# Four first loads on the ScalarE queue behind one memset, and another tile for the gate ahead of W_in

## The chip, the core and the metric

The kernel runs on one core of a Trainium2 chip. A core has TensorE (matrix products), VectorE, ScalarE, GpSimd and SyncE, which work side by side, each through its own instructions in order, and which wait for one another through semaphores. Sixteen DMA engines move data between the chip's memory (HBM) and the on-chip SBUF. SyncE and ScalarE issue DMAs through a hardware queue each, GpSimd through a software queue; all three run on the same sixteen DMA engines. The metric is the time of one execution on the device in microseconds (us), given as the median of several runs.

## The reference

A gated linear recurrence gives the input of a feed-forward layer. All inputs are float32: q, k, v and alpha are 4 x 8 x 768 x 48 (batch, heads, sequence, width of a head), W_in is 384 x 2048, W_out is 2048 x 384.

```python
for t in range(S):
    state = alpha[:, :, t, :, None] * state + np.einsum('bhd,bhe->bhde', k[:, :, t], v[:, :, t])
    y[:, :, t] = np.einsum('bhd,bhde->bhe', q[:, :, t], state)
...
x = y.transpose(0, 2, 1, 3).reshape(B * S, H * D)
h = x @ w_in
g = 0.5 * h * (1.0 + np.tanh(c * (h + 0.044715 * h * h * h)))
out = g @ w_out
```

## The kernel before

**Tiling.** The sequence is cut into 6 chunks of 128 tokens. A chunk of one batch entry is a unit; two units make a pair, and there are 12 pairs, two for each chunk. In a chunk the recurrence is written as an attention with a running product of alpha: ScalarE takes the logarithm of alpha (`ln`, L359), TensorE sums it over the tokens by a product with a triangular matrix (`cum`, L346 to L380), ScalarE makes the exponentials `b` and `binv` and the decay at the chunk's end `bend`, VectorE multiplies q by b and k by binv (`qp` and `kp`, L418). TensorE transposes both (`t`, L428), ScalarE or VectorE copies the result to SBUF (`ev`, L446), TensorE forms the products of q and k (`attn`, L489), VectorE masks them (`mask`, L496), TensorE multiplies by v (`y`, L543 and L546), and the state is carried on (`kv`, `st`). The output of a unit is transposed (`tx`, `xe`) and goes into layer 1 (`l1`, L572, product with W_in), GELU on ScalarE (L578) and layer 2 (`l2`, L591, product with W_out).

**Names.** `qp0.1` is the second `qp` of pair 0, and so on; `l10.3` is step 3 of layer 1 of block 0. A step of layer 1 covers two of the 16 column tiles of W_in, so steps 0 and 1 read part 0 of W_in, 2 and 3 part 1, 4 and 5 part 2, 6 and 7 part 3.

**Order.** A planner puts the tasks of each engine in order with costs and due times, but up to about the middle of pair 3 the order is written out by hand in the string `FIRST`: `A:ln0.0` means "ScalarE, next, ln0.0", with P, V, G and S for TensorE, VectorE, GpSimd and SyncE. Layer 1 of block 0 stands there in the order l10.0, l10.1, l10.3, l10.2, l10.5, l10.4, l10.6, l10.7, between the steps of pair 1. The planner's table of landing times (`LANDED`) is written out too. Each engine runs its instructions in that order.

**Loads.** The alpha, q and k of pairs 0 and 1 are loaded unit by unit through the hardware queues, 192 KB each: the table `RINGS` numbers them load.0 to load.11 (0 and 1 are alpha of pair 0, unit 0 and 1; 2 and 3 are q and k of unit 0; 4 and 5 are q and k of unit 1; 6 and 7 alpha of pair 1; 8 and 9 q and k of its unit 0; 10 and 11 those of its unit 1). Those in `BY_ACT` are issued by ScalarE, the others by SyncE. Everything else (v, W_in in 4 parts, W_out in 4 parts, and all loads from pair 2 on) goes through GpSimd's queue in the order of `LOADS`. A "gate" in that list is a copy of one element of a loaded tile by GpSimd (L314): GpSimd's queue stands until that tile has landed. `gatea 0 1` stands ahead of v of pair 0 and reads alpha of pair 0, unit 1; `gatek 0 1` stands ahead of W_in part 0 and reads k of pair 0, unit 1. Behind it in GpSimd's queue are W_in part 0, v of pair 1, W_in parts 1 to 3, W_out parts 0 and 1, and the loads of pair 2.

SyncE's last four loads of pair 1 each also wait until an earlier hardware load has landed, since they use its semaphore again: load.8 waits for load.0, load.9 for load.1, load.10 and load.11 for the third and the fourth hardware load of the program's order.

`run` (L865) first fills constants on VectorE and GpSimd and then emits the tasks in the order.

Of the kernel before, what the change touches and what calls it, by code (L numbers as in the profile page):

```python
# [7 lines left out]
F32 = mybir.dt.float32  # L8
# [163 lines left out]
class _Kernel:  # L172
# [3 lines left out]

    SPLIT = (2,)
    EARLY = (0, 1)
    LOADS = ('gatea 0 1', 'v0', 'gatek 0 1', 'in 0', 'v1', 'in 1', 'in 2', 'in 3', 'out 0', 'out 1', '2a', 'out 2', '2b', 'out 3', '3', '4', '5', '6', '7', '8', '9', '10', '11')

    PACKED, CUM_FF, R = (0, 1), (0, 1), 4
    RINGS = (('a', 0, 0, 1), ('a', 0, 1, 2), ('q', 0, 0, 1), ('k', 0, 0, 1), ('q', 0, 1, 2), ('k', 0, 1, 2),
             ('a', 1, 0, 1), ('a', 1, 1, 2), ('q', 1, 0, 1), ('k', 1, 0, 1), ('q', 1, 1, 2), ('k', 1, 1, 2))
    BY_ACT = (2, 3,)

    FIRST = """
        A:table.0 A:load.2 A:load.3 S:load.0 S:load.1 S:load.4 A:ln0.0 S:load.5 P:fill.7 P:cum0.0 A:ln0.1 G:gate.0 G:load.12 S:load.6 P:cum0.1 A:b0.0 S:load.7
        A:bend0.0 V:qp0.0 A:binv0.0 A:binv0.1 S:load.8 V:kp0.0 P:fill.2 P:t0.0 A:b0.1 V:ev0.0 P:fill.1 P:t0.1 S:load.9 A:ev0.1 V:qp0.1 S:load.10 A:bend0.1
        P:fill.3 P:attn0.0 V:kp0.1 G:gate.1 S:load.11 P:t0.2 G:load.13 V:mask0.0 A:ev0.2 P:t0.3 G:load.14 V:mask0.1 A:ev0.3 P:fill.1 P:t0.4 V:ev0.4 P:fill.1
        P:attn0.1 A:ln1.0 G:load.15 P:t0.5 V:mask0.3 P:cum1.0 A:ev0.5 G:load.16 V:vb0.0 A:ln1.1 V:end0.0 P:y0.0 V:mask0.2 G:load.17 P:kv0.0 A:binv1.0 P:cum1.1  # L190
# [428 lines left out]
    def tasks(self):  # L619
# [30 lines left out]
        for r, m, lo, hi in self.RINGS:  # L650
            loads[r, m, lo] = loads[r, m, hi - 1] = s.add(
                "load", {"ACT" if n in self.BY_ACT else "SP": W["ring_issue"]}, n, self.load(r, *pairs[m], lo, hi), land=(W["ring_v" if r == "v" else "ring"] * (hi - lo) // 2 if n else W["begin"]))
            n += 1
        for step in self.LOADS:
            if step[0] == "v":
# [209 lines left out]
    def run(self):  # L865
        nc, C = self.nc, self.C
        self.tasks()
        nc.vector.memset(self.zero, 0.0)
        nc.vector.memset(self.ones, 1.0)
        make_upper_triangular(nc, self.ut_h, val=1.0, diag=True)  # L870
        make_identity(nc, self.ident)
        nc.vector.memset(self.half, 0.0)
        for o in range(2):
            nc.vector.memset(self.half[64 * o:64 * o + 64, o:o + 1], 1.0)
        nc.vector.tensor_reduce(self.blk, self.ident.rearrange("p (g j) -> p j g", j=4), axis=mybir.AxisListType.X, op=ALU.max)
        same = self.blk[:, None, :].to_broadcast([C, C // 4, 4])
        nc.vector.tensor_tensor(self.ut_blk[1].rearrange("p (g j) -> p g j", j=4), self.ut_h.rearrange("p (g j) -> p g j", j=4), same, op=ALU.mult)
        nc.vector.tensor_tensor(self.ut_blk[0], self.ut_blk[1], self.ident, op=ALU.subtract)
        for i in range(max(self.BUFS[n] for n in self.ring)):
            for n in self.ring:  # L880
                if i < self.BUFS[n]:
                    nc.vector.memset(self.ring[n][i][:, :, :, self.D:64], 0.0)
        nc.vector.tensor_copy(self.ut, self.ut_h)
        order = self.s.order()
        for t in order:
            if t.load == LN_EXP:
                self.act_set(LN_EXP)
            t.emit(t.engine)
# [30 lines left out]
```

## Time and profile before

| | us |
|---|---|
| median of 9 runs | 177.43 |
| lowest and highest run | 176.85, 178.6 |
| the profiled execution | 176.79 |
| its span, first to last instruction | 175.0 |

TensorE's clock was granted in full (mean 1.000). The page lists each engine's busy time in the span, the chain of work that ended last, and the groups of instructions. An engine's busy share is an average over the whole span; for a change at the start the timeline of the start has to be read. In it, the landings of the first loads, as issue plus time to landing:

| load | issued by | issue, us | to landing, us | landed |
|---|---|---|---|---|
| alpha, pair 0, unit 0 | SyncE | 0.74 | 3.1 | 3.8 |
| q, pair 0, unit 0 | ScalarE | 0.77 | 3.5 | 4.3 |
| k, pair 0, unit 0 | ScalarE | 1.52 | 5.4 | 6.9 |
| q, pair 0, unit 1 | SyncE | 2.20 | 5.2 | 7.4 |
| k, pair 0, unit 1 | SyncE | 2.85 | 5.1 | 7.95 |
| v, pair 0 | GpSimd | 5.14 | 6.5 | 11.6 |
| k, pair 1, unit 0 | SyncE | 5.48 | 6.0 | 11.5 |
| W_in, part 0 | GpSimd | 8.53 | 6.0 | 14.5 |

From about 3 us on the DMA engines are busy nearly all the time (the share of them that is busy is 0.88 to 1.26 in every microsecond from 3 to 14; it can pass 1 because packets overlap).

### The profile page before, as it was taken

To read this page: it belongs to the slowest core of one execution; us is meant where nothing else is said; L and a number is where in the kernel's file an instruction comes from. 1 tells how busy PE (TensorE), PEld (TensorE's weight loads), DVE (VectorE), ACT (ScalarE), POOL (GpSimd) and SP (SyncE) were. 2 spreads that over 40 slices of the span, in tenths; PEclk is the share of its full clock that TensorE was granted. 3 is DMA by queue.
4 is the path that set the end of the run, shared out by engine and by line. 5 is a ranking of instruction groups with operands and counts; after the bars stand their busy time and mean duration, and the time that the engine had idled before them with its cause. 6 is when DMAs were issued, how large, how long until landed. Compare 5 with 4: busy or idle time off the path is not lost.

```text
span 175.0 us, 4439 instructions
## 1 busy us (share of the span) xinstructions
PE 169.9 (97%) x1845; PEld 134.9 (77%) x1845; DVE 96.5 (55%) x191; ACT 128.7 (74%) x213; POOL 57.6 (33%) x64
## 2 busy tenths in 40 slices
PE   7899999999999999999999999999999999999993
PEld 2567998667987896897798698698697697796973
DVE  6599820357888993895697997485426405000000
ACT  4677999666978668669788967977988984481941
POOL 2497348986645766566720000000000000000000
PEclk9999999999999999999999999999999999999999
DMA  4999999999999999999999993261270360401102
GB/s 140 294 269 227 209 244 234 242 208 208 250 263 194 248 251 218 226 226 198 193 275 218 194 153 102 59 171 43 47 187 28 90 165 4 119 16 49 45 0 90
DMA packets 49620, 28.86 MB, mean 165 GB/s; under 512 B 37696, under 2 KB 46016, under 8 KB 49600
## 3 DMA queue, kind: packets, MB, share of 16 engines
q0 software_dynamic: 26464, 17.70, 61.2%
q1 hardware_dynamic: 22592, 10.49, 24.8%
q10 hardware_dynamic: 544, 0.39, 0.8%
q8 instruction: 14, 0.23, 0.6%
q14 instruction: 6, 0.05, 0.1%
HBM read 25.17 MB, written 4.72 MB: 171 GB/s over the span
## 4 chain that ended last, share of the span: by engine, by line
PE 92%; DMA 3%; DVE 1%; ACT 1%; issue 1%; DVEq 0%
PE hT L572 36%; PE acc L591 36%; PE at L489 4%; PE qkT_ps L428 4%; DMA k<-in_k_dram 3%; PE yps L546 3%; PE kv L506 2%; PE yps L543 2%; PE cum L378 2%; PE xT_ps L560 1%; PE cum L380 1%; ACT qkT L446 1%; PE idle L289 1%; DVE kp L418 1%; PE k_ps L454 0%
## 5 line engine op out<-in xcount | busy, mean ns | idle before, releaser
L572 PE MATMUL hT<-xT,w_in 128*128 128x256 bf16 x576 | 69.4, 273 | 0.0
L578 ACT ACTIVATE gT<-hT 128x512 bf16<-128x512 f32 x96 | 56.3, 600 | 17.7 <-PE hT L572 14.3
L591 PE MATMUL acc<-w_out,gT 128*128 128x384 bf16 (+3 forms) x416 | 69.0, 313 | 0.0
L572 PEld LDWEIGHTS <-w_in 128*128 128x128 bf16 x576 | 61.1, 113 | 1.6
L591 PEld LDWEIGHTS <-gT 128*128 128x128 bf16 x416 | 36.9, 97 | 19.2
L496 DVE TENSOR_TENSOR atm<-at,ut 128x512 bf16<-128x512 f32 x48 | 30.1, 683 | 12.7 <-PE at L489 12.6
L418 DVE TENSOR_TENSOR qp<-q,b 128x768 bf16<-128x768 f32 (+1 forms) x15 | 11.9, 796 | 13.4 <-ACT b L407 13.4
L418 DVE TENSOR_TENSOR kp<-k,binv 128x768 bf16<-128x768 f32 (+1 forms) x15 | 11.9, 792 | 11.1 <-ACT binv L407 10.6
L603 ACT COPY ot<-acc 128x384 f32<-128x384 f32 (+3 forms) x17 | 7.4, 439 | 13.0 <-PE acc L591 12.9
L308 POOL DMA_DIRECT2D k<-in_k_dram x11 | 12.2, 1107 | 8.2 <-DMA vb<-in_v_dram 2.5
L308 POOL DMA_DIRECT2D a<-in_alpha_dram x11 | 12.2, 1114 | 5.7 <-DMA w_in<-in_moe_w_in_dram 1.4
L308 POOL DMA_DIRECT2D vb<-in_v_dram x11 | 12.1, 1104 | 5.6 <-PE qkT_ps L428 1.4
L308 POOL DMA_DIRECT2D q<-in_q_dram x11 | 12.2, 1108 | 5.4 <-DMA w_out<-in_moe_w_out_dram 1.0
L407 ACT ACTIVATE b<-cum 128x768 bf16<-128x768 f32 (+1 forms) x15 | 10.3, 684 | 3.2 <-PE cum L380 2.3
L280 ACT ACT_TABLE_LOAD x9 | 11.5, 1283 | 0.9 <-PEq L903 0.7
L578 ACT ACT_TABLE_LOAD x9 | 11.5, 1283 | 0.2
L407 ACT ACTIVATE binv<-cum 128x768 bf16<-128x768 f32 (+1 forms) x15 | 10.2, 681 | 0.2 <-PE cum L350 0.2
L528 DVE TENSOR_TENSOR stmp<-kv,st 128x384 f32<-128x384 f32 x16 | 8.9, 553 | 2.1 <-PE kv L506 2.0
L446 ACT COPY qkT<-qkT_ps 128x512 bf16<-128x512 bf16 (+1 forms) x9 | 6.5, 728 | 4.0 <-PE qkT_ps L428 4.0
L553 DVE CAST x<-yps 128x384 bf16<-128x384 f32 x12 | 6.7, 557 | 4.9 <-PE yps L546 4.9
L531 DVE TENSOR_TENSOR st<-stmp,ends 128x384 bf16<-128x384 f32 x16 | 8.9, 558 | 0.6
L546 PE MATMUL yps<-vb,atm 128*128 128x48 bf16 x192 | 8.7, 183 | 0.1
(64 smaller groups left out, 155.1 us busy)
## 6 DMA issues: line engine op xcount, KB each, us to landing
out_dram<-ot SPq DMA_DIRECT2D x19, 192.0 KB, 5.4
a<-in_alpha_dram POOLq DMA_DIRECT2D x9, 384.0 KB, 12.2
q<-in_q_dram POOLq DMA_DIRECT2D x9, 384.0 KB, 11.6
k<-in_k_dram POOLq DMA_DIRECT2D x9, 384.0 KB, 11.8
vb<-in_v_dram POOLq DMA_DIRECT2D x9, 192.0 KB, 11.7
w_in<-in_moe_w_in_dram POOLq DMA_DIRECT2D x4, 384.0 KB, 8.3
w_out<-in_moe_w_out_dram POOLq DMA_DIRECT2D x4, 384.0 KB, 11.0
out_dram<-ot SPq DMA_DIRECT2D x9, 96.0 KB, 1.8
```

The source lines that it names most:

```text
L280: nc.scalar.add_instruction(mybir.InstLoadActFuncSet(name=nc.get_next_instruction_name(), act_func_set_id=i, engine=mybir.EngineType.Activ ...
L308: dma(u[t][:, lo:hi].rearrange("t b h d -> t (b h) d"), src.rearrange("b h s d -> s (b h) d")[c * C:(c + 1) * C])
L407: self.nc.scalar.activation(u[n].rearrange("t i h d -> t i (h d)")[:, lo:hi], cum, AF.Exp, scale=1.0 if n == "b" else -1.0)
L418: self.nc.vector.tensor_tensor(out, rows, b, op=ALU.mult)
L446: self.copy(e)(t, ps)
L496: self.nc.vector.tensor_tensor(u["atm", i][:, o], u["at", i][o], self.ut[:, None, :].to_broadcast([self.C, self.H // 2, self.C]), op=ALU.mult)
L528: nc.vector.tensor_tensor(s, acc, old, op=ALU.add)
L531: nc.vector.tensor_tensor(new.rearrange("f p (o d) -> f (p o) d", o=2), acc.rearrange("f p (o d) -> f (p o) d", o=2), ends, op=ALU.mult)
L546: nc.tensor.matmul(y[:, h, :], u["atm", i][:, h % 2, h // 2, :], u["vb"][:, i, h, :], start=c == 0, stop=True, skip_group_check=True)
L572: self.nc.tensor.matmul(h[:, s], w_in[:, j, nt % 4 + s], self.xT[c % self.NX][:, j, lo:hi].rearrange("p g t -> p (g t)"), start=j == 0, st ...
L578: return lambda e: self.nc.scalar.activation(self.gT[c % self.NG][:, nt:nt + 2, lo * self.C:hi * self.C], f.pop(("h", c, lo, nt)), AF.Gelu ...
L591: self.nc.tensor.matmul(f["acc", c, b][:, lo:hi], self.gT[c % self.NG][:, nt, b * self.C:(b + 1) * self.C], self.w_out[:, nt, lo:hi], star ...
```

## The change

Four things are edited.

- `BY_ACT` is (2, 3, 4, 5) instead of (2, 3), and `FIRST` begins with load.4 and load.5 on ScalarE: q and k of both units of pair 0 are now issued by ScalarE, right after its table load and ahead of ln0.0. SyncE issues the four alphas of pairs 0 and 1 one after another, and then q and k of pair 1.
- In `run` the tile of q of pair 0 is made before the planner's tasks, and VectorE writes a zero to one element of each partition of it, after the constants zero and ones. The first load into that tile therefore waits for this memset, and with it the three that stand behind it on ScalarE's queue.
- The gate ahead of W_in reads k of pair 1, unit 0 (`gatek 1 0`) instead of k of pair 0, unit 1.
- The semaphores used again follow the new order: load.10 now waits for q of pair 0, unit 0, and load.11 for k of pair 0, unit 0.

The order of instructions on TensorE, and the order of the rest on the other engines, is the same. (The lines behind the new ones count two further.)

```diff
-    LOADS = ('gatea 0 1', 'v0', 'gatek 0 1', 'in 0', 'v1', 'in 1', ...
+    LOADS = ('gatea 0 1', 'v0', 'gatek 1 0', 'in 0', 'v1', 'in 1', ...
...
-    BY_ACT = (2, 3,)
+    BY_ACT = (2, 3, 4, 5)
...
     FIRST = """
-        A:table.0 A:load.2 A:load.3 S:load.0 S:load.1 S:load.4 A:ln0.0 S:load.5 P:fill.7 P:cum0.0 A:ln0.1 G:gate.0 ...
+        A:table.0 A:load.2 A:load.3 A:load.4 A:load.5 S:load.0 S:load.1 A:ln0.0 P:fill.7 P:cum0.0 A:ln0.1 G:gate.0 ...
...
         make_upper_triangular(nc, self.ut_h, val=1.0, diag=True)
+        first = self.p[0, 0]["q"] = self.tile("q", [C, 2, self.H, self.D], F32)
+        nc.vector.memset(first[:, 0, 0, 0:1], 0.0)
         make_identity(nc, self.ident)
```

More of the change, by code (lines that the diff above doesn't have):

```diff
@@ L178 @@
     EARLY = (0, 1)
-    LOADS = ('gatea 0 1', 'v0', 'gatek 0 1', 'in 0', 'v1', 'in 1', 'in 2', 'in 3', 'out 0', 'out 1', '2a', 'out 2', '2b', 'out 3', '3', '4', '5', '6', '7', '8', '9', '10', '11')
+    LOADS = ('gatea 0 1', 'v0', 'gatek 1 0', 'in 0', 'v1', 'in 1', 'in 2', 'in 3', 'out 0', 'out 1', '2a', 'out 2', '2b', 'out 3', '3', '4', '5', '6', '7', '8', '9', '10', '11')
     PACKED, CUM_FF, R = (0, 1), (0, 1), 4
@@ L183 @@
              ('a', 1, 0, 1), ('a', 1, 1, 2), ('q', 1, 0, 1), ('k', 1, 0, 1), ('q', 1, 1, 2), ('k', 1, 1, 2))
-    BY_ACT = (2, 3,)
+    BY_ACT = (2, 3, 4, 5)
     FIRST = """
-        A:table.0 A:load.2 A:load.3 S:load.0 S:load.1 S:load.4 A:ln0.0 S:load.5 P:fill.7 P:cum0.0 A:ln0.1 G:gate.0 G:load.12 S:load.6 P:cum0.1 A:b0.0 S:load.7
+        A:table.0 A:load.2 A:load.3 A:load.4 A:load.5 S:load.0 S:load.1 A:ln0.0 P:fill.7 P:cum0.0 A:ln0.1 G:gate.0 G:load.12 S:load.6 P:cum0.1 A:b0.0 S:load.7
         A:bend0.0 V:qp0.0 A:binv0.0 A:binv0.1 S:load.8 V:kp0.0 P:fill.2 P:t0.0 A:b0.1 V:ev0.0 P:fill.1 P:t0.1 S:load.9 A:ev0.1 V:qp0.1 S:load.10 A:bend0.1
```

## The prediction

> **What bounds the kernel now.** I read the page's busy shares first, then the chain of waits (whole, and for the first 13.5 us), then timelines by engine up to 36 us, then the DMA view cut to short stretches.
>
> ```profile
> PE 169.9 (97%) x1845; PEld 134.9 (77%) x1845; DVE 96.5 (55%) x191; ACT 128.7 (74%) x213; POOL 57.6 (33%) x64
> PE 92%; DMA 3%; DVE 1%; ACT 1%; issue 1%; DVEq 0%
> ```
>
> TensorE is busy 97% of the 175.0 us span and is 92% of the chain that ended last; in the list of waits TensorE has one of 1.2 us at the very start, three of 0.2 to 0.3 up to 10 us, and none in the dense part. So whatever delays TensorE once its dense stretch has begun (about 16.5 us) comes out at the end undiminished, and only the first 23 us, where it still depends on loads, can change the time. The chain there:
>
> ```profile
> 0.74 0.75 ACT L280
> ...
> 1.52 5.39 DMA k<-in_k_dram
> ...
> 7.00 0.57 DVE kp L418
> 7.62 0.40 PE qkT_ps L428 x4
> ```
>
> Columns are start, length, piece. The one long load on the chain is k of unit 0 (ScalarE issues it at 1.52, it lands at 6.91). VectorE's kp stood ready 0.52 us for it. Then the gate and W_in on GpSimd, and the products that read W_in (start, length, engine, line; the bracket is idle time):
>
> ```profile
> 8.06 0.18 POOL L314 COPY gate<-k 128x1 f32<-128x1 f32 x1 [1.64 <-DMA k<-in_k_dram]
> 8.53 0.74 POOL L321 DMA_DIRECT2D w_in<-in_moe_w_in_dram  x1 [0.29 <-issue]
> 9.26 1.18 POOL L308 DMA_DIRECT2D v<-in_v_dram  x1
> 10.43 2.25 POOL L321 DMA_DIRECT2D w_in<-in_moe_w_in_dram  x3
> ```
>
> ```profile
> 16.52 0.82 PE L572 MATMUL hT<-xT,w_in 128*128 128x256 bf16 x6
> ...
> 19.14 0.83 PE L572 MATMUL hT<-xT,w_in 128*128 128x256 bf16 x6
> ...
> 19.97 1.47 PE L572 MATMUL hT<-xT,w_in 128*128 128x256 bf16 x12
> ...
> 22.48 6.71 PE L572 MATMUL hT<-xT,w_in 128*128 128x256 bf16 x60
> ```
>
> The DMA view by issue gives the landings: parts 0 to 3 of W_in take 6.0, 7.8, 8.9 and 10.0 us from issues at 8.53, 10.43, 11.18 and 11.93, so they land at 14.5, 18.2, 20.1 and 21.9. By the hand order l10.0 (16.52) is first to need part 0, l10.3 (19.14) part 1, l10.5 (the second six of the twelve at 19.97, so about 20.6) part 2, l10.6 (22.48) part 3. **The slack is 2.0, 0.9, 0.5 and 0.5 us.** That is the number this case turns on.
>
> **The change, part by part.**
>
> *The order of instructions.* TensorE's order is unchanged. VectorE gains one tiny memset near 1.15 us (the 128x1 memset of the ones took 0.06 us): it lies under the wait for alpha and costs nothing.
>
> *The hold.* Load q of unit 0 now waits for that memset, so ScalarE issues from about 1.2 us instead of 0.77. Alpha 0 loses its competitor for 0.4 us; alpha 1 no longer shares with q. I expect alpha 0 at about 3.5 (was 3.84) and alpha 1 at 4.4 to 4.9 (was 4.95).
>
> *Four issues on ScalarE instead of two.* Its two took 0.72 and 0.88 us; SyncE's take 0.61 to 0.74. Four from 1.2 us end between 3.6 (4 x 0.61) and 4.6 (0.72 + 3 x 0.88); I take 4.1, the middle, because each of its two rows overlapped one of SyncE's and the new ones overlap too. Queued behind them is ln of unit 0 (3.83 before): so about +0.3, between 0 and +0.75, and the earlier alpha is not used. Cover: binv of unit 0 ends at 6.33 and kp waits for k until 6.91, so 0.6 us of such a delay is hidden if k lands as before. If k came sooner, this would be late next.
>
> *Where q and k travel.* k of unit 0 stays the fourth load in order of issue; q and k of unit 1 fall from fifth and sixth to sixth and eighth, since SyncE now issues both alphas of pair 1 right after those of pair 0. The next rows are the two hardware queues in the stretch from 5 to 7 us, SyncE's q1 and ScalarE's q10:
>
> ```profile
> q1 hardware_dynamic: 715, 0.52, 86.0%
> q10 hardware_dynamic: 88, 0.06, 11.5%
> ```
>
> While k of unit 0 was still under way on ScalarE's queue, that queue moved 88 packets beside SyncE's 715. The Trainium skill (DMA: Bandwidth & Descriptors, "Issuing engines are not separate DMA queues") says that DMAs of several engines interleave on the same 16 engines, so spreading them saves only sequencer time. By that rule landing follows total bytes: the sixth and eighth landings of before, 7.95 and 9.07. By the row, ScalarE's queue may get less than its turn. Unit 1's q is used at 8.08 and k at 8.57. By the rule kp of unit 1 is 0.5 late; of that 0.4 hides where k's transposed copy on ScalarE (10.0) waits behind q's, leaving +0.1 to +0.2. By the row it may be 1 to 2 us late. Against that, k of unit 0 may come 0.2 to 0.6 earlier on its own queue. I take the head at +0.2, with ends of -0.4 and +2.0.
>
> *The new release of W_in.* The text in the code is "gatek 1 0": the tile read is k of pair 1, unit 0, on SyncE's queue. Before it landed at 11.5 (issue 5.48, 6.0 us) and the gate stood on k of unit 1 of pair 0, 7.95. In the new order ten loads of 0.197 MB and v of pair 0 (0.393 MB) stand up to it: 2.36 MB. Summing the GB/s of before by microsecond (123 from 2 us, then 356, 289, 261, 322, 321, 330, 301) that much is through at 10.2; landing lags the packets by 0.5 to 1.2. I take 10.9, ends 10.2 and 11.6. From landing to the issue of W_in took 0.58 (7.95 to 8.53), so part 0 is issued at 11.5 instead of 8.53: +3.0. Behind the gate in GpSimd's queue stand v of pair 1, W_in 1 to 3, W_out 0 and 1, and the loads of pair 2; all move with it.
>
> *How much of those 3.0 us comes back.* Part 0 took 6.0 us before, sharing with SyncE's queue until about 12.2. The Trainium skill (same page, "Anatomy of one DMA — SWDGE (gpsimd) path") gives about 2.0 us plus bytes over 436 GB/s; with the 0.786 MB read that is an estimate of 3.8 us. The rows say more: v of pair 0, issued at 5.14, showed its first packet at 8.25, and the landings of W_in parts are 1.85 us apart when nothing else runs. First packet 2.1 to 3.1 after the issue, 1.85 of packets, 0.5 of lag: 4.5 to 5.5. I take 4.7, nearer the short end because the queue is empty by then. Part 0 lands at 11.5 + 4.7 = 16.2, **1.7 later**; by the page it would be 15.3 and 0.8 later. The parts behind come back to back at the pace of before, so all are 1.7 late. The same seen from the engines: SyncE's loads end near 11.5 to 12 and W_in's first packet comes near 13.6, a hole of about 1.7 where before there was none.
>
> *The sum.* Part 1 stalls TensorE by 1.7 - 0.9 = 0.8, part 2 and part 3 raise this to 1.7 - 0.5 = 1.2. A late head moves the need for W_in by as much, so the two don't add: the larger counts, 1.2 against 0.2. By the page's figure it would be 0.8 - 0.5 = 0.3. v of pair 1 (16.7, first used at 18.07, slack 1.4) adds 0.3 at most, inside the same 1.2. W_out parts 0 and 1 have slack of 5.3 and about 3.3 and stay covered.
>
> The profiled execution took 176.79 us (175.0 of span and 1.8 around it): 176.79 + 1.2 = 178.0. The median of the nine runs, 177.43, is 0.64 above it, so the median to expect is 177.43 + 1.2 = **178.6 us**.
>
> **The rivals.**
>
> *Hidden.* k of pair 1 lands at 10.2 and a lone W_in load takes 3.8 to 4.3: part 0 is 0.1 to 0.6 late, within the slack of 0.5, and the head stays. 177.4. For it: the page's figure, and that alphas and rows reach SyncE's queue earlier. Against: v of pair 0 still shares the stretch before, and no load on GpSimd's queue in this trace landed in under 6.0 us.
>
> *ScalarE's queue is starved.* With up to eight loads on SyncE's queue, q and k of unit 1 come at the share shown above and land 2 us later (k at 10 or after). kp of unit 1, the second attention product, its mask, and v's cast behind it on VectorE move, and TensorE's dense part starts 1.5 to 2.0 later: 179.2. For it: 88 against 715. Against: by 7 us that was only the tail of one load.
>
> *Faster.* Place: kp of unit 0. With the alphas alone on the wire and k on a queue of its own, k lands by 6.3; ScalarE's four issues end by 3.7; kp starts 0.5 earlier and everything behind follows. Price: -0.5, 176.9; more isn't to be had, because binv ends at 6.33. It decides only if W_in is at most 0.0 us late, since an earlier head eats the slack of 0.5. For it: the 0.52 us wait at kp is real. Against: three conditions at once, one of them against the 3.0 us later issue.
>
> **How the numbers follow.** 0.3% is 0.53 us, about what a measurement of this kernel can tell from no change: 176.9 to 177.96. Forecast (W_in late, +0.6 to +2.5): 0.60. Hidden: 0.20, nearly all within 0.3%. Starved: 0.12. Faster: 0.08. Slower 0.71, same 0.21, faster 0.08. The range of 177.1 to 180.0 leaves out the faster case and a W_in more than 3 us late.
>
> **What would show it.** Right: the gate's copy starts near 11, W_in's first issue near 11.5, a dent in DMA share between 12 and 13.5, and TensorE waiting at hT for W_in at about 19 to 23 us, in sum near 1 us, with the rest unchanged and shifted. ln of unit 0 starts at 4.0 or later. Wrong: no wait on W_in; or kp of unit 1 well after 9.1, which is the starved case; or the gate before 10. If the gate's copy is near 11 and W_in still lands by 15, the term of 4.7 us was too large.

## The result, and the profile after

The changed kernel takes **179.02 us** (median of 18 runs, 178.42 to 179.94). The kernel before, run beside it and since, has a median of 177.23 us in 54 runs. The ratio is **1.0101, 95% interval 1.0081 to 1.0121**: 1.8 us slower. The forecast was 178.6 us, in a range of 177.1 to 180.0. The ratios below leave out two slow runs, 180.75 us in experiment 2 and 179.78 in experiment 6, each over 1.5% above the fastest of its kernel.

The page of the changed kernel, on an execution of 178.94 us: the span, TensorE's busy time, the hardware queues' packets, and the chain of waits by engine and line.

```profile
span 177.2 us, 4440 instructions
...
PE 170.1 (96%) x1845; PEld 135.0 (76%) x1845; DVE 96.5 (54%) x192; ACT 128.7 (73%) x213; POOL 58.0 (33%) x64
...
q1 hardware_dynamic: 22048, 10.10, 23.5%
q10 hardware_dynamic: 1088, 0.79, 1.4%
...
PE 90%; DMA 5%; DVE 1%; ACT 1%; issue 1%; SPq 0%
PE hT L572 36%; PE acc L591 34%; PE at L489 4%; PE qkT_ps L428 4%; DMA a<-in_alpha_dram 3%; PE yps L546 3%; DMA xT<-x 2%; PE kv L506 2%; PE yps L543 2%; PE cum L378 2%; PE xT_ps L560 1%; PE idle L289 1%; ACT qkT L446 1%; PE cum L380 1%; PE k_ps L454 0%
```

TensorE does the same work (170.1 us against 169.9), so the 2.2 us of longer span are waits. Two loads went over to ScalarE's queue (q10 has 1088 packets, and had 544). The long load on the chain is no longer k of unit 0 but an alpha. The next lines are GpSimd's timeline of the changed kernel (start, length, engine, line):

```profile
6.50 0.19 POOL L314 COPY gate<-a 128x1 f32<-128x1 f32 x1 [4.68 <-DMA a<-in_alpha_dram]
...
9.95 0.38 POOL L314 COPY gate<-k 128x1 f32<-128x1 f32 x1 [2.04 <-DMA k<-in_k_dram]
10.41 0.75 POOL L321 DMA_DIRECT2D w_in<-in_moe_w_in_dram  x1
11.15 1.18 POOL L308 DMA_DIRECT2D v<-in_v_dram  x1
12.33 2.26 POOL L321 DMA_DIRECT2D w_in<-in_moe_w_in_dram  x3
```

W_in part 0 is issued at 10.41 instead of 8.53. Parts 1 to 3, with 7.7, 8.8 and 10.0 us to landing from 12.33, 13.08 and 13.84, land at 20.0, 21.9 and 23.8: 1.8 to 1.9 later than before. TensorE's timeline of the changed kernel shows what that does, and one wait far behind:

```profile
17.66 0.81 PE L572 MATMUL hT<-xT,w_in 128*128 128x256 bf16 x6
...
20.28 0.83 PE L572 MATMUL hT<-xT,w_in 128*128 128x256 bf16 x6
...
21.11 1.66 PE L572 MATMUL hT<-xT,w_in 128*128 128x256 bf16 x12
...
23.83 6.74 PE L572 MATMUL hT<-xT,w_in 128*128 128x256 bf16 x60
...
102.65 0.82 PE L572 MATMUL hT<-xT,w_in 128*128 128x256 bf16 x6 [0.70 <-DMA xT<-x]
```

Layer 1 begins 1.14 late (17.66 against 16.52), and l10.6, the first to need part 3, 1.35 late (23.83 against 22.48). The 0.21 added on the way are W_in: the twelve products at 21.11 take 1.66 instead of 1.47, and l10.6 begins at the landing of part 3 (23.8), though no bracket shows a wait. Read by itself, this page seems to say that the late second alpha made most of the loss and W_in little. The alpha (ScalarE's `ln`, the idle time in the bracket):

```profile
6.47 0.52 ACT L359 ACTIVATE la<-a 128x384 f16<-128x384 f32 x1 [2.02 <-DMA a<-in_alpha_dram]
```

It had started at 4.99. So two theories stood after this page. **Two-limits theory:** the gate costs the time, as forecast; in this execution a late head (the work ahead of layer 1) merely lay beside it, since a late head moves the need for W_in too and only the larger of the two counts. **Head theory:** the moved issues delay the second alpha, and that is the cost. Beside them, the forecast's rule (lateness of part 3 less its slack of 0.5) could be tested by doses.

### The profile page after: what moved, and what is told of

Read it like the earlier page. It is cut to its first block, busy times and chain, and to the rows that moved or that the text cites. A ratio compares the mean times of both kernels' runs of the same rounds, so it can differ in the third digit from the quotient of the medians.

```text
span 177.2 us, 4440 instructions
## 1 busy us (share of the span) xinstructions
PE 170.1 (96%) x1845; PEld 135.0 (76%) x1845; DVE 96.5 (54%) x192; ACT 128.7 (73%) x213; POOL 58.0 (33%) x64
## 3 DMA queue, kind: packets, MB, share of 16 engines
q10 hardware_dynamic: 1088, 0.79, 1.4%
## 4 chain that ended last, share of the span: by engine, by line
PE 90%; DMA 5%; DVE 1%; ACT 1%; issue 1%; SPq 0%
PE hT L572 36%; PE acc L591 34%; PE at L489 4%; PE qkT_ps L428 4%; DMA a<-in_alpha_dram 3%; PE yps L546 3%; DMA xT<-x 2%; PE kv L506 2%; PE yps L543 2%; PE cum L378 2%; PE xT_ps L560 1%; PE idle L289 1%; ACT qkT L446 1%; PE cum L380 1%; PE k_ps L454 0%
## 5 line engine op out<-in xcount | busy, mean ns | idle before, releaser
L578 ACT ACTIVATE gT<-hT 128x512 bf16<-128x512 f32 x96 | 56.4, 599 | 18.8 <-PE hT L572 15.3
L280 ACT ACT_TABLE_LOAD x9 | 11.5, 1283 | 0.9 <-PEq L905 0.7
L578 ACT ACT_TABLE_LOAD x9 | 11.5, 1283 | 0.2
## 6 DMA issues: line engine op xcount, KB each, us to landing
w_out<-in_moe_w_out_dram POOLq DMA_DIRECT2D x4, 384.0 KB, 10.9
```

Of the source, the lines that this page charges most:

```text
L280: nc.scalar.add_instruction(mybir.InstLoadActFuncSet(name=nc.get_next_instruction_name(), act_func_set_id=i, engine=mybir.EngineType.Activ ...
L578: return lambda e: self.nc.scalar.activation(self.gT[c % self.NG][:, nt:nt + 2, lo * self.C:hi * self.C], f.pop(("h", c, lo, nt)), AF.Gelu ...
```

## The experiments

All ratios are to the kernel before on the same chip, with 95% intervals.

**1. The gate alone.** The kernel before, no issue moved, nothing held:

```diff
-    LOADS = (... 'gatek 0 1', 'in 0', ...
+    LOADS = (... 'gatek 1 0', 'in 0', ...
```

> The kernel before with the one edit at the gate: W_in waits for k of pair 1, unit 0. Two-limits theory (the later of the head and of W_in sets the time): the head is as before (second ln at about 5.0, kp at 7.0), the gate opens near 11.3, W_in is issued near 11.8 and each part lands 2.3 to 3 later, so TensorE waits for W_in by 1.8 to 2.5 in sum: 179.0 to 179.7, as slow as the changed kernel or slower. Head theory (the late second alpha alone costs the time, W_in is covered): no change from before.

Measured: 179.98 us, ratio 1.0171 (1.0132 to 1.0209), the slowest of all. GpSimd's and TensorE's timelines of this kernel:

```profile
10.82 0.18 POOL L314 COPY gate<-k 128x1 f32<-128x1 f32 x1 [4.43 <-DMA k<-in_k_dram]
11.28 0.74 POOL L321 DMA_DIRECT2D w_in<-in_moe_w_in_dram  x1 [0.29 <-issue]
```

```profile
17.62 0.85 PE L572 MATMUL hT<-xT,w_in 128*128 128x256 bf16 x6 [0.93 <-DMA w_in<-in_moe_w_in_dram]
...
21.60 0.85 PE L572 MATMUL hT<-xT,w_in 128*128 128x256 bf16 x6 [1.17 <-DMA w_in<-in_moe_w_in_dram]
...
23.48 0.84 PE L572 MATMUL hT<-xT,w_in 128*128 128x256 bf16 x6 [0.21 <-DMA w_in<-in_moe_w_in_dram]
...
26.03 6.20 PE L572 MATMUL hT<-xT,w_in 128*128 128x256 bf16 x55 [0.50 <-DMA w_in<-in_moe_w_in_dram]
```

Here the alphas and k of pair 0 are about as early as before, or earlier, and TensorE waits 2.8 us for W_in in four places; its list of waits names no other load. The span is 178.5: 3.5 longer, and l10.6 is 3.55 late. The head theory, which had expected no change, falls as the only cause. The time even lies above the range expected.

**2. The changed kernel with the old gate.** The same line the other way round.

> The changed kernel with the old gate: W_in waits for k of pair 0, unit 1, which landed at 8.85. Two-limits theory: the second alpha still lands at 6.4, so the head is 1.1 late, W_in is issued near 9.5 and is about 0.9 late, covered: TensorE starts layer 1 near 17.65 and the sum is +1.1 over before (178.3), only 0.2 to 0.3 under the changed kernel. W_in theory (the gate alone costs the time): back within 0.3 of before.

Measured: 178.02 us, ratio 1.0065 (1.0039 to 1.0090). By its size (+1.1) this is the number of the two-limits theory, but not by its reason: in the profiled execution, at 177.1 the lowest of the 14, the second alpha landed at 4.9 and layer 1 began at 16.45, no later than before. The stricter theory, that the old gate brings the time back within 0.3, is refuted. A second execution of each of the two kernels was profiled.

> The changed kernel with the old gate once more, one look, because the first look's time (177.1) was the lowest of 14. At the usual 178.0 the trace should show what the first one did not: the second alpha at 6 or later or k of unit 1 after 9 (head theory), or W_in parts 2 and 3 about 1 late and TensorE waiting for them (W_in theory), or a wait for a transposed x near 100.

This execution took 178.42. ScalarE's and GpSimd's timelines of it:

```profile
5.64 0.52 ACT L359 ACTIVATE la<-a 128x384 f16<-128x384 f32 x1 [1.19 <-DMA a<-in_alpha_dram]
```

```profile
9.30 0.18 POOL L314 COPY gate<-k 128x1 f32<-128x1 f32 x1 [2.22 <-DMA k<-in_k_dram]
9.76 0.74 POOL L321 DMA_DIRECT2D w_in<-in_moe_w_in_dram  x1 [0.28 <-issue]
```

k of unit 1, now last in ScalarE's queue, lands 1.2 later than before (9.2 against 7.95). The old gate stands on that very tile, so W_in is late here too (9.76 against 8.53) and TensorE waits 0.7 us for it at l10.3 and l10.5. Layer 1 itself begins at 17.16, 0.64 late. Head and W_in are both late in this execution; W_in is the later one, since l10.6 begins (24.18) when part 3 lands (24.1).

> The changed kernel once more, one look. If the late second alpha (6.4) belongs to the change: it lands at 6.0 to 6.5 again. If it is a matter of one execution: at 4.9 to 5.1, with W_in's parts still 1.5 to 2 late and the time 178.4 to 179.4 all the same.

Measured 179.6 us. TensorE's timeline of this second execution of the changed kernel:

```profile
17.40 0.81 PE L572 MATMUL hT<-xT,w_in 128*128 128x256 bf16 x6
18.50 0.82 PE L572 MATMUL hT<-xT,w_in 128*128 128x256 bf16 x6
20.92 0.84 PE L572 MATMUL hT<-xT,w_in 128*128 128x256 bf16 x6 [0.74 <-DMA w_in<-in_moe_w_in_dram]
21.77 0.82 PE L572 MATMUL hT<-xT,w_in 128*128 128x256 bf16 x6
22.87 0.84 PE L572 MATMUL hT<-xT,w_in 128*128 128x256 bf16 x6 [0.28 <-DMA w_in<-in_moe_w_in_dram]
23.76 0.83 PE L572 MATMUL hT<-xT,w_in 128*128 128x256 bf16 x6
25.30 6.74 PE L572 MATMUL hT<-xT,w_in 128*128 128x256 bf16 x60 [0.38 <-DMA w_in<-in_moe_w_in_dram]
```

Same instructions, another picture: the second alpha was there at 5.25 instead of 6.4, W_in was issued at 10.92, and TensorE waited 1.4 us for W_in. The alpha at 6.4 was a matter of one execution; the late W_in was there in both. The two are coupled: k of pair 1, on which the gate stands, uses the semaphore of the second alpha again, and it was issued right behind that alpha's landing, at 6.47 in the first execution and at 5.27 in the second.

**3. W_in released early in the changed kernel.** If the moved issues cost anything by themselves, it must be left when W_in is early.

```diff
-    LOADS = (... 'gatek 1 0', 'in 0', ...
+    LOADS = (... 'gatek 0 0', 'in 0', ...
```

> The changed kernel with W_in released by k of pair 0, unit 0 (lands near 6.5 to 6.9), so that W_in is early and only the head is left. Two-limits theory: layer 1 starts 0 to 1.1 late as the second alpha lands early or late in that execution, TensorE never waits for W_in, sum +0.6 to +1.1 over before (177.5 to 178.1). If W_in is all of it: equal to before within 0.3. A new competitor (W_in's packets beside q and k of unit 1) could add: then kp of unit 1 after 9.5 and +1.5.

Measured: **177.29 us, ratio 1.0009 (0.9985 to 1.0033)**: nothing measurable is left of the loss. TensorE's list of waits (us in total, times, longest) and GpSimd's issue in this kernel:

```profile
PE idle L289 <- DVE half L874: 1.2, 1, 1.2
PE k_ps L454 <- ACT qkT L446: 0.5, 1, 0.5
PE cum L346 <- ACT la L359: 0.4, 1, 0.4
PE yps L546 <- DVE vb L389: 0.2, 1, 0.2
PE qkT_ps L428 <- DVE xT L564: 0.2, 1, 0.2
```

```profile
7.92 0.74 POOL L321 DMA_DIRECT2D w_in<-in_moe_w_in_dram  x1
```

No wait for W_in. The execution profiled was the slowest of 13, though (178.9 us, with layer 1 beginning at 18.7), and so late a head needs W_in later: the parts landed at 15.5 to 23.1, each 1.0 to 1.2 later than in the kernel before. So the trace doesn't show an early W_in, and the verdict rests on the median: one edit at the gate, with all moved issues and the hold in place, takes the loss away.

**4. The same early release in the kernel before.**

> The kernel before with the same earlier release of W_in. W_in is covered before already (slack 0.5), so an earlier W_in gains nothing: 0 to +0.3 over before by more sharing for q and k of pair 1. If W_in's slack is often used up in executions other than the profiled one: -0.2 to -0.5.

Measured: 177.34 us, ratio 1.0010 (0.9984 to 1.0036). An earlier issue of W_in gains nothing. That W_in was covered is only a part of it. In the profiled execution (177.93 us, 0.6 above the median) the issue at 7.34 did not bring an earlier landing: part 0 took 8.0 us instead of 6.0 and landed at 15.3, part 3 at 23.6, and the last k on SyncE's queue took 8.5 us instead of 4.5. TensorE waits for W_in here:

```profile
19.88 0.84 PE L572 MATMUL hT<-xT,w_in 128*128 128x256 bf16 x6 [0.33 <-DMA w_in<-in_moe_w_in_dram]
...
21.74 0.85 PE L572 MATMUL hT<-xT,w_in 128*128 128x256 bf16 x6 [0.20 <-DMA w_in<-in_moe_w_in_dram]
```

**5. One load less at the gate, in both kernels.** `gateq 1 0`, which reads q of pair 1, unit 0.

> The changed kernel with W_in released by q of pair 1, unit 0, one load earlier in SyncE's queue than k. Dose theory (the time follows the moment at which W_in is issued, once that is past about 8.5 to 9): W_in issued near 9.9 to 10.3, +1.2 to +1.5 over before, 0.2 to 0.6 under the changed kernel. If the moved issues make the time and the gate does not: as the changed kernel, +1.7 to +2.0.

Measured: 178.15 us, ratio 1.0046 (1.0026 to 1.0065); W_in issued at 9.75.

> The kernel before, only with W_in released by q of pair 1, unit 0. No issue is moved and nothing is held. Dose theory: q lands near 9.3, W_in is issued near 9.8, +0.9 to +1.4 over before. If the moved issues are needed for a loss: 0 to +0.3.

Measured: 178.34 us, ratio 1.0067 (1.0049 to 1.0085); W_in issued at 9.70, and TensorE waits for it twice:

```profile
19.58 0.85 PE L572 MATMUL hT<-xT,w_in 128*128 128x256 bf16 x6 [0.23 <-DMA w_in<-in_moe_w_in_dram]
...
21.51 0.84 PE L572 MATMUL hT<-xT,w_in 128*128 128x256 bf16 x6 [0.26 <-DMA w_in<-in_moe_w_in_dram]
...
23.42 6.74 PE L572 MATMUL hT<-xT,w_in 128*128 128x256 bf16 x60
```

The loss appears with no issue moved.

**6. The hold and the moved issues, one by one.** The memset alone in the kernel before:

> The kernel before with the memset that holds q of unit 0, and nothing else. If the hold is what throws the second alpha behind q (q then travels beside it instead of beside the first alpha): second alpha at 6.0 to 6.5, +1.0 to +1.2 (178.3). If the moved issues do it: second alpha at 4.9 to 5.0, no change (177.2 to 177.5).

Measured: 177.06 us, ratio 1.0012 (0.9993 to 1.0030), second alpha at 4.8: the hold costs nothing. The other way round, the changed kernel without the memset:

> The changed kernel without the memset: nothing holds ScalarE's first issue. If the hold does nothing by itself: +1.6 to +2.0 over before, as the changed kernel. If the hold protects the alphas, or hurts them: 0.4 or more away from it.

Measured: 179.13 us, ratio 1.0094 (1.0071 to 1.0117): as the changed kernel. And the moved issues alone, with the old gate and no hold:

> The kernel before with q and k of unit 1 issued by ScalarE, no hold, old gate. If the hold is the cause of the late second alpha: second alpha at 4.9 to 5.1 and a head within 0.3 of before, 177.2 to 177.6, with k of unit 1 at 8.5 to 9. If the moved issues are the cause (the alphas of pair 1 right behind on SyncE's queue): second alpha at 6.0 to 6.5 and +1.0 to +1.2.

Measured: 178.12 us, ratio 1.0077 (1.0049 to 1.0105), second alpha at 5.1. Neither branch of what was expected: no late alpha, and yet slower. k of unit 1 lands at 9.3, VectorE waits for it, the gate opens at 9.42 and W_in goes out at 9.88:

```profile
9.42 0.49 POOL L314 COPY gate<-k 128x1 f32<-128x1 f32 x1 [2.86 <-DMA k<-in_k_dram]
9.88 0.74 POOL L321 DMA_DIRECT2D w_in<-in_moe_w_in_dram  x1
```

**7. A try at a better start.**

```diff
-    BY_ACT = (2, 3,)
+    BY_ACT = (1, 2)
...
-        A:table.0 A:load.2 A:load.3 S:load.0 S:load.1 S:load.4 ...
+        A:table.0 A:load.1 A:load.2 S:load.0 S:load.3 S:load.4 ...
```

> Not the change, but a try at a better start: the kernel before with the second alpha and q of unit 0 on ScalarE's queue, and k of unit 0 second on SyncE's. Both alphas go out at 0.75, so the second one should land near 4.3 instead of 4.95; k of unit 0 is third. If the head's length is set by the loads' order: -0.2 to -0.5 against before. If the wait at kp only moves to another load of the four: within 0.3.

Measured: 177.20 us, ratio 1.0019 (0.9998 to 1.0041). The second alpha came at 4.1, the first at 4.5, and nothing was gained. None of the kernels tried beats the one before.

**The doses side by side** (moments in us, of the profiled executions; the ratio is of the medians):

| kernel | issues moved | W_in issued | part 3 landed | l10.6 began | ratio |
|---|---|---|---|---|---|
| before, gate on k of pair 0, unit 0 | no | 7.34 | 23.6 | 23.65 | 1.0010 |
| changed, the same gate | yes | 7.92 | 23.1 | 24.67 | 1.0009 |
| hold alone | no | 8.08 | 22.5 | 22.57 | 1.0012 |
| second alpha on ScalarE (experiment 7) | other ones | 8.19 | 21.7 | 23.92 | 1.0019 |
| before | no | 8.53 | 21.9 | 22.48 | 1 |
| changed, old gate, first execution | yes | 8.96 | 22.7 | 22.73 | 1.0065 |
| changed, old gate, second execution | yes | 9.76 | 24.1 | 24.18 | 1.0065 |
| before, gate on q of pair 1 | no | 9.70 | 23.4 | 23.42 | 1.0067 |
| changed, gate on q of pair 1 | yes | 9.75 | 23.3 | 23.36 | 1.0046 |
| moved issues alone | yes | 9.88 | 23.2 | 23.27 | 1.0077 |
| changed, first execution | yes | 10.41 | 23.8 | 23.83 | 1.0101 |
| changed, second execution | yes | 10.92 | 25.2 | 25.30 | 1.0101 |
| changed without the hold | yes | 10.99 | 24.4 | 24.48 | 1.0094 |
| gate alone | no | 11.28 | 26.0 | 26.03 | 1.0171 |

Up to 8.5 us the moment of W_in's issue makes no measurable difference. From there the time goes up by 0.7 to 1.4 us for each us, whether issues were moved or not. In eleven of the fourteen executions l10.6 begins within 0.1 us of the landing of part 3, in all those with W_in issued after 8.6 us among them. Behind l10.6 nothing changes: in all fourteen the span ends 152.5 to 152.7 us later, once the wait at 102 us (below) is taken off. So where W_in goes out late, the landing of its last part sets the time.

The moved issues don't add to the gate's loss: the whole change is faster than the gate alone, 1.0101 against 1.0171, with intervals apart. With two loads fewer ahead of it on SyncE's queue, k of pair 1 landed at 9.8 and 10.3 instead of 10.7. Whether that is the whole of the difference was not tried.

## Why the prediction was right

The cause was right: the gate on k of pair 1, with TensorE waiting for W_in at layer 1. Experiment 1 gives the loss with the gate alone and experiment 3 takes it away with the gate alone.

- **The hold costs nothing**: right (1.0012, interval across 1).
- **ScalarE's four issues**: they ended at 3.9 against 4.1 taken, since each took 0.63 to 0.70. `ln` of unit 0 began 0.10 later, not 0.3. It did wait for the issues, as forecast, though the bracket names alpha: it began at 3.93 or 3.94 in all six executions with the hold and four issues, wherever alpha landed between 3.6 and 3.8, and the last issue ended at 3.89.
- **The alphas**: wrong for the second. The first landed at 3.7 and 3.6, 0.1 to 0.2 earlier, where 0.3 was expected; the second at 6.4 and 5.25 in two executions of the changed kernel against 4.95, and was to come earlier.
- **q and k of unit 1**: by the Trainium skill's rule (DMA: Bandwidth & Descriptors, "Issuing engines are not separate DMA queues") they were to land at 7.95 and 9.07; they landed at 8.1 and 8.85 in the first execution, at 8.7 and 9.2 in the second. The row of 88 packets against 715 had suggested a starved queue. From 4.5 to 6.5 us ScalarE's queue now moved 354 packets and SyncE's 345: it was not starved, the row had been the tail of one load. The rule was the better guide, though not a sure one: in the profiled execution of experiment 3 they landed at 9.2 and 10.1, and the head was 2.2 late.
- **The head at +0.2**: too small for the executions seen (layer 1 began 1.14 and 0.88 late) and about right for the median of experiment 3, where the whole left-over is 0.2 us. Executions differ by more than that.
- **The gate**: predicted 10.9 for k's landing and 11.5 for W_in's issue, measured 9.8 and 10.4 in one execution, 10.3 and 10.9 in the other.
- **Issue to landing of a lone W_in part**: taken as 4.7, measured 4.9 and 5.2. With the gate alone it was 6.3, and there nothing of the later issue came back: issued 2.75 later, part 0 landed 3.1 later. The same page's fit ("Anatomy of one DMA — SWDGE (gpsimd) path"), an estimate of 3.8, was too short, and with it the rival called "hidden".
- **The sum**: right as a rule. Part 3's lateness less its slack of 0.5 gives 1.9 - 0.5 = 1.4 in the first execution (l10.6 1.35 late), 3.3 - 0.5 = 2.8 in the second (2.82 late, span 2.8 longer). That only the larger of head and W_in counts was seen in the first: 1.14 of head, and 1.35 in all.
- **The signs named beforehand**: taken alone, the first profile counts against the forecast: the gate's copy at 9.95 (before 10), no wait for W_in in the list, kp of unit 1 at 9.73. The second bears it out: the copy at 10.45, 1.4 us of waits, DMA engines busy 0.41 and 0.38 of the time from 11 to 13 us.

**The term that was mis-sized** is "the parts behind come back to back at the pace of before, so all are 1.7 late". Part 0 made up for 0.8 to 1.1 of the later issue, where 1.3 was forecast (it landed 0.8 and 1.6 late), but from part 0 to part 1, with v of pair 1 between, 4.7 us passed instead of 3.7, in both executions. Parts 1 to 3 were then 1.8 to 1.9 late in one and 2.6 to 3.3 in the other. The pace of before was that of one execution: 3.7 is the shortest of the fourteen, which range up to 5.4, and the hold alone, with the loads in the order of before, shows 4.5. Why it varies stays open. The issue was earlier than forecast and the stream slower, and the errors partly cancelled, which was luck. The measured 1.8 us lie half above the 1.2 of the sum.

Not foreseen at all is the wait of 0.70 us for a transposed x at 102 us. Waits of 0.4 to 0.6 at that place stand in three other kernels with moved issues; the second execution of the changed kernel and those with the old gate have none. In the four with the wait, SyncE's issue of the transpose of q just ahead took 2.2 to 2.4 us, in place of 1.8 before. Why it does so in some executions was not tried and stays open. The 1.1 us of the kernel with the old gate go with W_in for the most part: in both its executions l10.6 began when part 3 landed, and with W_in released early (experiment 3) 0.2 us are left of them, 0.6 at most by the interval.

## What to carry to other kernels

A gate that holds back a stream of loads is priced at the first use of each load behind it. Write down landing, first use and slack for every part: the smallest slack (here 0.5 us, the last parts) is all that the gate may move, however much room the first part has. A slack is that of one execution: with the hold alone part 3 landed right at its use (22.5 and 22.57), without a measurable loss. And take a second profile, or undo one edit, before believing one page. The two profiles of the changed kernel put the loss in different places, while the cause was the same.

## What the runs showed of the hardware

**The first products run slow until the full clock is granted.** TensorE's first sum over alpha, seven products, took from 0.82 to 1.44 us, by no edit. The kernel before, and the kernel before with the gate on q:

```profile
4.41 0.82 PE L346 MATMUL cum<-la,ut_blk 128*128 128x384 f16 x7
```

```profile
4.39 1.44 PE L346 MATMUL cum<-la,ut_blk 128*128 128x384 f16 x7
```

The row of the granted clock reads 1.00 in that microsecond in both, but it counts the time ahead of the first entry in the trace's clock record as full. That entry, the grant of the full clock, comes at 4.21 us in the first of these executions and at 5.86 in the second. The others agree: with the grant at 4.47, 4.96, 5.19, 5.46 and 5.60 the sum took 0.82, 1.03, 1.18, 1.32 and 1.33 us, and with later ones 1.41 to 1.44. In the twelve executions with such an entry it lies between 4.2 and 9.9 us. The Trainium skill (TensorE: Matmul & The Clock Gate, "What's actually happening") says that a warm-up whose length varies between runs precedes the full rate, and the trace agrees. In the pair shown, the slow sum moved qp of unit 0 from 5.92 to 6.47, but not kp (7.00 and 6.95), which had been waiting for k, nor layer 1 (16.52 and 16.57). The two executions with the latest grant, at 8.6 and 9.9, are also those in which layer 1 began latest (17.96 and 18.70); what the clock and what the loads have in that was not separated.

**Landings of one load scatter by more than a microsecond.** The second alpha, issued at 1.5 us on the same queue with the same neighbours, landed at 4.8, 4.9, 5.25, 5.6, 5.8 and 6.4 in the six profiled executions whose first issues are those of the changed kernel, while the first alpha and q of unit 0, landing ahead of it, stayed within 0.3 us. In the five that leave the issues of before where they were, or only hold q, it landed at 4.8 to 5.5. Whether the moved issues make a late alpha more likely is open.
